# Reordering the start of the second stage of a convolution and spectral-mixing kernel

## The chip, the cores and the metric

The kernel runs on one core of one Trainium2 chip. The metric is device microseconds of that core, the median over the runs shown. A second number, the span, is the time from the first to the last instruction of one profiled execution.

## What is computed

Eight sequences of 3264 positions with 192 channels pass through a causal convolution of 7 taps (softmaxed weights, one set per head of 24 channels), then through a spectral layer that changes only the lowest 64 frequencies, and at last through a residual product with `w_ch`:

```python
x = attn(x, weight)                       # causal 7-tap convolution, per head
X = np.fft.rfft(x, axis=1)[:, :64]
Yr = einsum('bmd,mde->bme', Xr, w_r) - einsum('bmd,mde->bme', Xi, w_i)
Yi = einsum('bmd,mde->bme', Xr, w_i) + einsum('bmd,mde->bme', Xi, w_r)
y = np.fft.irfft(Y, n=S, axis=1)
u = x + y
out = u + np.maximum(u @ w_ch, 0.0)
```

## The kernel before, in words

The eight sequences are taken as four pairs, q = 0 to 3, and each sequence as 25 tiles of 128 positions (t = 0 to 24) and a half tile of 64. The program order is written out by hand, and every engine works its own queue in that order.

**Stage one** loads the inputs, convolves, transforms to 64 frequencies, and lays transposed copies of the convolved tiles into `cc`. The mixing follows: `mix(g)` (lines 430 to 441), for g = 0 to 15, multiplies four frequencies with their weights, which arrive by DMA. Its sums go to two of the four one-bank PSUM tiles `low[0]` to `low[3]`. `mix_copy` (ScalarE) takes them to SBUF, `mix_trans` transposes them into `low[2]` and `low[3]`, one bank for each half of the channels, and VectorE (the first half) and ScalarE (the second half) copy these into `yet`, the mixed spectrum.

**Stage two** is a list of items, `duos`, in the order in which they are worked. An ordinary item is a pair of output tiles for the two sequences of a q: 128 partitions and 768 columns in a PSUM tile of two banks. There are four such double tiles, and item n uses number n modulo 4. An item goes through these steps:

- `c_part` (line 488): twelve matmuls of 192 columns, the product of `cc` with `w_ch`. Its first matmul starts the accumulation, so the double tile must have been emptied of item n - 4 by then.
- `m_part(n, 0)` (line 508): the inverse transform of Y W added to it, which gives u W.
- `relu` (line 534): ScalarE, in place in PSUM.
- `m_part(n, 1)`: the inverse transform of Y added, so that PSUM holds relu(u W) + y.
- `finish` (line 559): VectorE adds x from `xall` and writes one of six output buffers in `arena`; then the output DMA is issued, on SP's queue (line 567: one DMA of 384 KB where the item is one t of two q; line 572: two of 192 KB where it is two t of one q).

Four items are not ordinary. Three of them, called Y W here, prepare the spectrum of q = 1, 2, 3: `zw_part` (line 515) multiplies `yet` by `wm` and `w1` and gives, side by side, Y W (192 columns) and Y itself (192 columns, a product with an identity matrix, part of which is zero columns); `zw_copy` scales both into `zw`. The Y W of q = 0 is done ahead of the loop, in the `low` tiles. The fourth is `"h"`, the half tiles of all sequences, written by four DMAs on POOL's queue (line 548).

The loop (lines 616 to 630) is a software pipeline. At step n it issues `m_part(n, 0)` and `relu(n)`, then `c_part(n + 1)` or the Y W that stands at n + 1, then `m_part(n - 1, 1)` and `finish(n - 1)`. Items 0 and 1 have their `c_part` ahead of the loop, item 0 behind the last mixing and item 1 behind the Y W of q = 0. The Y W items stand at places 2, 15 and 21 of the list, and `"h"` at 23. The four ring tiles of stage one close ahead of the last mixing, which frees the double tiles 0 and 1 (`za`); all four `low` tiles close behind the first Y W, which frees the double tiles 2 and 3 (`zb`).

Of the kernel before, what the change touches and what calls it, by code (L numbers as in the profile page):

```python
# [12 lines left out]
F32 = mybir.dt.float32  # L13
BF16 = mybir.dt.bfloat16
# [5 lines left out]
def kernel(  # L20
# [9 lines left out]
    nc = tc.nc  # L30
    B, S, D = x.shape
    H, KK = weight.shape
    MODES = moe_w_r.shape[0]
# [3 lines left out]
    P = 128  # L37
    NQ = B // 2
    NF = S // P
# [13 lines left out]
    def sb(name, shape, dtype, **kw):  # L53
        return pool.tile([P] + shape, dtype, tag=name, name=name, **kw)
# [15 lines left out]
    yet = sb("yet", [2, 2 * MODES, B], BF16)  # L70
# [3 lines left out]
    zw = mixa[:, 0:4 * NQ * D].rearrange("p (q c t d) -> p q c t d", q=NQ, c=2, t=2)  # L74
    band = sb("band", [H, 2 * P], BF16)
    wm = sb("wm", [2 * D], BF16)
    w1 = sb("w1", [2 * D], BF16)
# [12 lines left out]
    def wbuf(g):  # L90
        return wts[g] if g < NW + NL else wts[(g - NW - NL) % NW]
# [35 lines left out]
    def psum_pool(name, side):  # L127
        stack = ExitStack()
        return stack, stack.enter_context(tc.tile_pool(name=name, bufs=1, space=PSUM, side=side))

    conv_stack, pp = psum_pool("pconv", "left")
    Z = [pp.tile([P, 2, 512], F32, tag=f"z{i}", name=f"z{i}") for i in range(2)]
    low_stack, pp = psum_pool("plow", "right")
    low = [pp.tile([P, 512], F32, tag=f"low{i}", name=f"low{i}") for i in range(4)]

    def slot(q, t):
        return NT * q + t
# [265 lines left out]
    for k, u in enumerate(units):  # L403
# [5 lines left out]
        if k:  # L409
            q, t0, n = units[k - 1]  # L410
# [8 lines left out]
    NG = MODES // 4  # L419

    def load_w(g):
        if g < NG:
            for half, src in ((0, moe_w_r), (1, moe_w_i)):
                nc.gpsimd.dma_start(out=wbuf(g)[64 * half:64 * half + 64, :, :, :],  # L424
                                    in_=src[4 * g:4 * g + 4, :, :].rearrange("m (p j) e -> p m j e", j=3))
# [4 lines left out]
    def mix(g):  # L430
        yp = low[(g // 2) % 2][:, D * (g % 2):D * (g % 2) + D]
        for j in range(3):
            for p4 in range(4):
                m = 4 * g + p4
                nc.tensor.matmul(yp[32 * p4:32 * p4 + 2 * B, :], xt[:, j, :, m],  # L435
                                 wbuf(g)[:, p4, j, :], start=(j == 0), stop=(j == 2),
                                 tile_position=(0, 32 * p4), skip_group_check=True)
        if g < NW:
            load_w(g + NW + NL)
        elif g >= NW + NL:  # L440
            load_w(g + NW)
# [3 lines left out]
                       in_=low[d % 2][:, 0:2 * D].rearrange("p (g d) -> p g d", g=2)[:, gs, :])  # L445

    def mix_trans(d, gs=slice(0, 2)):
        ets = [low[2 + t][:, :].bitcast(BF16)[:, 0:2 * P].rearrange("p (g k) -> p g k", g=2) for t in range(2)]
        for t in range(2):
            for g in range(gs.start, gs.stop):  # L450
                nc.tensor.transpose(ets[t][:, g, :], ymix[d % 2][:, g, 64 * t:64 * t + P], ident[:])
        m = slice(8 * d + 4 * gs.start, 8 * d + 4 * gs.stop)
        for t in range(2):
            dst = yet[:, t, :, :].rearrange("p (c m) b -> p m c b", c=2)[:, m, :, :]
            srcv = ets[t][:, gs, :].rearrange("p g (q k) -> p (g q) k", q=4)[:, :, 0:16].rearrange(
                "p m (c b) -> p m c b", c=2)
            if t == 0:
                nc.vector.tensor_copy(out=dst, in_=srcv)
            else:
                nc.scalar.copy(out=dst, in_=srcv)  # L460

    conv_stack.close()
    ring_stack, pp = psum_pool("pring", "left")
# [6 lines left out]

    ROWS = (LO, UP)

    def c_part(n):
        duo, zt = items[n]
        if duo[0] == "h":
            for a in range(2):
                for j in range(3):
                    for k in range(2):
                        for i, r in enumerate(ROWS):
                            h = ROWS[i ^ k]  # L480
                            nc.tensor.matmul(zt[h, k, D * a:D * a + D], cc[r, 2 * k + a, 3 * NF + j, h], wc[r, j, :],
                                             start=(a == 0 and j == 0), stop=False, skip_group_check=True,
                                             tile_position=(r.start, h.start))
            return
        for k, (q, t) in enumerate(duo):
            for j in range(3):
                for i, r in enumerate(ROWS):
                    nc.tensor.matmul(zt[:, i, D * k:D * k + D], cc[r, q, 3 * t + j, :], wc[r, j, :],  # L488
                                     start=(k == 0 and j == 0), stop=False, skip_group_check=True)

    def m_part(n, which):

        duo, zt = items[n]
        for c in range(2):
            end = which == 1 and c == 1
            if duo[0] == "h":
                for k in range(2):
                    for i, r in enumerate(ROWS):
                        h = ROWS[i ^ k]
                        nc.tensor.matmul(zt[h, k, 0:2 * D], tabs[c][r, NF, 0:HALF], zw[r, 2 * k:2 * k + 2, c, which, :],  # L500
                                         start=False, stop=end, skip_group_check=True,
                                         tile_position=(r.start, h.start))
                continue
            (q0, t0), (q1, t1) = duo[0], duo[-1]
            parts = [(0, 2, q0, t0)] if t0 == t1 and q0 != q1 else [(k, 1, q, t) for k, (q, t) in enumerate(duo)]
            for k, w, q, t in parts:
                for i, r in enumerate(ROWS):
                    nc.tensor.matmul(zt[:, i, D * k:D * (k + w)], tabs[c][r, t, :], zw[r, q:q + w, c, which, :],  # L508
                                     start=False, stop=end and k + w == len(duo), skip_group_check=True)

    def zw_part(q, c, z):

        for t, w in enumerate((wm, w1)):
            for i, r in enumerate(ROWS):
                nc.tensor.matmul(z[r, 0:2 * D], yet[:, t, MODES * c:MODES * c + MODES, 2 * q + i], w[:],  # L515
                                 start=(t == 0), stop=(t == 1), tile_position=(0, 64 * i), skip_group_check=True)

    def zw_copy(dst, src, act):
        if act:
            nc.scalar.activation(out=dst, in_=src, func=ACT.Copy, scale=ascale[:, 0:1])  # L520
        else:
            nc.vector.tensor_scalar(out=dst, in0=src, scalar1=ascale[:, 0:1], scalar2=None, op0=ALU.mult)

    duos = [((q, t), (q, t + 1)) for q in range(2) for t in (0, 2)]
    duos += [((q, t), (q + 1, t)) for q in (0, 2) for t in range(0 if q else 4, NF)]

    duos[-1:] = [(u,) for u in duos[-1]]
    for k, item in ((2, 1), (15, 2), (21, 3), (23, ("h",))):
        duos.insert(k, item)

    def relu(n):
# [42 lines left out]
    N = len(duos)  # L574
    items = [[duo, None] for duo in duos]

    def assign(Z):
        for k, item in enumerate(items):
            if k % 4 in Z:
                item[1] = Z[k % 4]  # L580
# [14 lines left out]
    stack, pp = psum_pool("pz0", "left")  # L595
    ctx.push(stack)
    assign({k: pp.tile([P, 2, 512], F32, tag=f"za{k}", name=f"za{k}") for k in (0, 1)})
    mix(NG - 1)
    mix_copy(NG // 2 - 1, slice(1, 2))
    c_part(0)  # L600
    mix_trans(NG // 2 - 1, slice(1, 2))
    for c in range(2):
        zw_part(0, c, low[2 * c])
    for w in range(2):
        for c in range(2):
            zw_copy(zw[:, 0, c, w, :], low[2 * c][:, D * w:D * w + D], c)
    c_part(1)
    low_stack.close()
    stack, pp = psum_pool("pz1", "right")
    ctx.push(stack)  # L610
    assign({k: pp.tile([P, 2, 512], F32, tag=f"zb{k}", name=f"zb{k}") for k in (2, 3)})

    def is_duo(n):
        return 0 <= n < N and isinstance(duos[n], tuple)

    for n in range(N + 1):
        if is_duo(n):
            m_part(n, 0)
            relu(n)
        if n + 1 < N and n > 0:  # L620
            if is_duo(n + 1):
                c_part(n + 1)
            else:
                q, zt = items[n + 1]
                for c in range(2):
                    zw_part(q, c, zt[:, c, :])
                zw_copy(zw[:, q, :, :, :].rearrange("p c t d -> p c (t d)"), zt[:, :, 0:2 * D], q > 1)
        if is_duo(n - 1):
            m_part(n - 1, 1)
            finish(n - 1)  # L630


# [28 lines left out]
```

## Time and profile before

| what | value |
|---|---|
| median of 6 runs | 181.64 us (181.36 to 187.92) |
| the profiled execution | 181.42 us |
| its span | 179.7 us |
| TensorE busy in the span (PE) | 147.3 us, 82% |
| VectorE busy (DVE) | 112.0 us, 62% |
| ScalarE busy (ACT) | 98.4 us, 55% |
| stage two, first `c_part` to the last VectorE add | about 107.9 to 174.2 us |
| one ordinary item in the steady part | about 1.15 us |
| bytes written | 20.05 MB |

The profiled execution takes 1.7 us more than its span; that part lies outside the first and last instruction. Times in the views count from the start of the span. In a timeline row the columns are start, length, engine, source line, operation, output and inputs, shapes, number of instructions, and in brackets how long the engine stood idle before the row and who released it. Several instructions that follow one another are merged into one row. PEld rows are weight loads, which run beside matmuls.

### The profile page before, as it was taken

Reading aid. Unit: us, or ns where it says so; the run is one execution under the profiler, and the core shown is the slowest. Engines: PE = TensorE matmul, PEld = TensorE weight load, DVE = VectorE, ACT = ScalarE, POOL = GpSimd, SP = SyncE. Lnnn points to the kernel's source line nnn. Section 1 sums busy time; section 2 is a strip of 40 time slices with the busy share of each in tenths; the row PEclk is TensorE's granted clock in tenths of the full one; section 3 lists DMA queues with packets and bytes.
Section 4 is the critical chain, followed back from the end, with each engine's and each line's share of the span. In section 5 each row is a group of like instructions: output and inputs, shape, how many; then the busy total and the mean of one; then the engine's idle time right before and its main releaser. Section 6 shows DMA issues by size and latency. Waiting matters only on the chain.

```text
span 179.7 us, 6296 instructions
## 1 busy us (share of the span) xinstructions
PE 147.3 (82%) x2736; PEld 108.9 (61%) x2736; DVE 112.0 (62%) x159; ACT 98.4 (55%) x134; POOL 68.8 (38%) x113
## 2 busy tenths in 40 slices
PE   0047879999999997894776769999999999999940
PEld 0033556666667665673565657888776778888830
DVE  1878574866866683442435352788766878888870
ACT  8076646544554634163454455466776666666630
POOL 7999998768975644443334000000000500000000
PEclk9999999999999999699999999999999999999995
DMA  4999999999999999999999950469989699999995
GB/s 48 159 176 188 190 190 190 191 191 192 189 191 190 207 204 207 209 204 207 206 207 206 207 93 4 139 226 365 348 283 314 186 326 370 365 355 350 333 371 170
DMA packets 62875, 40.17 MB, mean 224 GB/s; under 512 B 28800, under 2 KB 62784, under 8 KB 62848
## 3 DMA queue, kind: packets, MB, share of 16 engines
q0 software_dynamic: 36224, 20.08, 80.4%
q1 hardware_dynamic: 26624, 19.69, 32.6%
q8 instruction: 21, 0.34, 0.8%
q14 instruction: 6, 0.05, 0.1%
HBM read 39.40 MB, written 20.05 MB: 331 GB/s over the span
## 4 chain that ended last, share of the span: by engine, by line
DMA 37%; PE 35%; POOL 19%; issue 3%; DVE 2%; ACT 1%; POOLq 0%; DVEq 0%
DMA arena<-in_moe_w_i_dram 18%; POOL xall L145 14%; DMA xall<-in_x_dram 13%; PE za L508 9%; PE zb L508 8%; PE za L488 8%; DMA cc<-in_moe_w_i_dram 7%; PE zb L488 6%; DVE arena L559 2%; POOL xall L215 1%; POOL arena L424 1%; PE zb L515 1%; ACT xall L321 1%; DVE arena L554 1%; PE low L435 1%
## 5 line engine op out<-in xcount | busy, mean ns | idle before, releaser
L145 POOL DMA_DIRECT2D xall<-in_x_dram x48 | 38.5, 813 | 4.7 <-DMA xall<-in_x_dram 2.3
L303 PE MATMUL z<-xall,band 64*64 64x192 bf16 (+3 forms) x816 | 27.4, 264 | 14.5 <-ACT band L189 10.5
L323 DVE CAST xall<-z 128x768 bf16<-128x768 f32 (+1 forms) x24 | 24.5, 1021 | 13.9 <-PE z L303 12.1
L303 PEld LDWEIGHTS <-band 64*64 64x64 bf16 x816 | 18.4, 110 | 22.9 <-ACT band L189 10.9
L321 ACT CAST xall<-z 128x768 bf16<-128x768 f32 (+1 forms) x24 | 20.4, 851 | 20.5 <-PE z L303 19.1
L488 PEld LDWEIGHTS <-cc 64*128 64x128 bf16 x600 | 27.0, 94 | 6.6 <-issue 1.7
L559 DVE TENSOR_TENSOR arena<-za,xall 128x768 f32<-128x768 f32 x26 | 24.8, 956 | 6.1 <-ACT za L534 2.0
L534 ACT ACTIVATE za<-za 128x768 f32<-128x768 f32 (+1 forms) x27 | 21.0, 783 | 9.5 <-PE za L508 9.5
L559 DVE TENSOR_TENSOR arena<-zb,xall 128x768 f32<-128x768 f32 x23 | 21.9, 956 | 6.3 <-ACT zb L534 2.9
L534 ACT ACTIVATE zb<-zb 128x768 f32<-128x768 f32 (+1 forms) x25 | 19.6, 782 | 10.1 <-PE zb L508 8.6
L329 PE MATMUL low<-xall,ftab 128*128 128x384 bf16 x100 | 22.0, 348 | 0.0
L383 PEld LDWEIGHTS <-xall 128*128 128x128 bf16 x300 | 18.5, 104 | 3.2 <-issue 0.3
L358 DVE COPY cc<-r 128x1024 bf16<-128x1024 bf16 (+1 forms) x16 | 10.2, 670 | 14.6 <-ACT xs L444 6.2
L548 POOL DMA_DIRECT2D out_dram<-arena x4 | 2.4, 615 | 42.4 <-DVE arena L540 42.4
L488 PE MATMUL za<-wc,cc 64*128 64x192 bf16 x318 | 17.9, 243 | 0.4 <-DVE arena L559 0.4
L508 PE MATMUL za<-mixa,ftab 64*128 64x384 bf16 (+1 forms) x120 | 18.1, 304 | 0.0
L508 PE MATMUL za<-mixa,fsin 64*128 64x384 bf16 (+1 forms) x120 | 18.1, 304 | 0.0
L508 PE MATMUL zb<-mixa,ftab 64*128 64x384 bf16 (+1 forms) x100 | 16.1, 313 | 0.4 <-ACT zb L534 0.4
L508 PE MATMUL zb<-mixa,fsin 64*128 64x384 bf16 (+1 forms) x100 | 16.1, 313 | 0.0
L488 PE MATMUL zb<-wc,cc 64*128 64x192 bf16 x282 | 15.8, 243 | 0.0
L356 ACT COPY cc<-r 128x1024 bf16<-128x1024 bf16 (+1 forms) x9 | 8.9, 989 | 10.0 <-PE r L383 8.9
L508 PEld LDWEIGHTS <-ftab 64*128 64x128 bf16 x220 | 11.8, 94 | 3.9 <-issue 1.5
(108 smaller groups left out, 185.0 us busy)
## 6 DMA issues: line engine op xcount, KB each, us to landing
out_dram<-arena SPq DMA_DIRECT2D x45, 384.0 KB, 4.4
xall<-in_x_dram POOLq DMA_DIRECT2D x24, 192.0 KB, 6.9
xall<-in_x_dram POOLq DMA_DIRECT2D x16, 240.0 KB, 6.5
arena<-in_moe_w_r_dram POOLq DMA_DIRECT2D x12, 288.0 KB, 9.2
arena<-in_moe_w_i_dram POOLq DMA_DIRECT2D x12, 288.0 KB, 10.0
out_dram<-arena SPq DMA_DIRECT2D x10, 192.0 KB, 2.8
xall<-in_x_dram POOLq DMA_DIRECT2D x8, 144.0 KB, 6.1
cc<-in_moe_w_r_dram POOLq DMA_DIRECT2D x4, 288.0 KB, 11.2
```

Of the source, the lines that this page charges most:

```text
L145: nc.gpsimd.dma_start(out=xall[:, s0:s0 + nf, i, :], in_=src)
L303: mm = nc.tensor.matmul(ov[c], band[r, h, c.start + shift + 64 * (r is UP and c is LO): c.start + shift + 64 * (r is UP and c is LO) + 64] ...
L321: nc.scalar.copy(out=dst, in_=srcv)
L323: nc.vector.tensor_copy(out=dst, in_=srcv)
L329: nc.tensor.matmul(xp, ftab[:, t, :], xall[:, slot(q, t), :, :], start=(t == 0), stop=False, skip_group_check=True)
L356: nc.scalar.copy(out=out, in_=in_)
L358: nc.vector.tensor_copy(out=out, in_=in_)
L383: nc.tensor.transpose(tp[:, P * k:P * k + P], src, ident[:])
L488: nc.tensor.matmul(zt[:, i, D * k:D * k + D], cc[r, q, 3 * t + j, :], wc[r, j, :], start=(k == 0 and j == 0), stop=False, skip_group_check ...
L508: nc.tensor.matmul(zt[:, i, D * k:D * (k + w)], tabs[c][r, t, :], zw[r, q:q + w, c, which, :], start=False, stop=end and k + w == len(duo) ...
L534: nc.scalar.activation(out=zt[:, :, 0:w], in_=zt[:, :, 0:w], func=ACT.Relu)
L559: nc.vector.tensor_tensor(out=o[:, :, :].rearrange("p k (i d) -> p i k d", i=2), in0=zt[:, :, 0:2 * D].rearrange("p i (k d) -> p i k d", k=2),
```

## The change

The diff does six things.

1. The `low` tiles are held in two pools, one with `low[1]` and `low[3]`, one with `low[0]` and `low[2]`. The second closes ahead of the last mixing, so that double tile 2 is there already; the first closes where all four closed. Only double tile 3 waits for it.
2. The transposes of the last pair of mixings put both halves of the channels into `low[3]`, side by side. The Y W of q = 0 uses `low[1]` and `low[3]`.
3. Half of `c_part(1)` (its first tile, six matmuls) is put ahead of the Y W of q = 0, the other half and the whole `c_part(2)` behind it. Before, the whole `c_part(1)` stood behind it.
4. `zw_part` leaves out the columns that are zero: three matmuls of 320, 192 and 64 columns in place of two of 384, for each of the four combinations of c and i. That makes twelve for eight, and 576 columns for 768.
5. `zw_copy` in the loop is done in two halves, Y W on VectorE and Y on ScalarE, where one instruction on one engine did both.
6. Six items, not four, take two t of one q (t = 0 to 5 of q = 0 and 1). The Y W items stand at places 3, 8 and 10, and `"h"` at 13. The loop begins with `m_part(0, 0)`, `m_part(1, 0)`, `m_part(2, 0)`, the Y W of q = 1, and only then `m_part(0, 1)` and `m_part(1, 1)`, each with its `finish`; the step behind them is `c_part(4)`.

```diff
-    low_stack, pp = psum_pool("plow", "right")
-    low = [pp.tile([P, 512], F32, tag=f"low{i}", name=f"low{i}") for i in range(4)]
+    low = [None] * 4
+    low_stacks = []
+    for odd in (1, 0):
+        stack, pp = psum_pool(f"plow{odd}", "right")
+        low_stacks.append(stack)
+        for i in (odd, odd + 2):
+            low[i] = pp.tile([P, 512], F32, tag=f"low{i}", name=f"low{i}")
...
-        ets = [low[2 + t][:, :].bitcast(BF16)[:, 0:2 * P].rearrange("p (g k) -> p g k", g=2) for t in range(2)]
+        ets = [(low[3][:, P * t:P * t + P] if d == NG // 2 - 1 else low[2 + t][:, 0:P]).bitcast(BF16).rearrange(
+            "p (g k) -> p g k", g=2) for t in range(2)]
...
-        for t, w in enumerate((wm, w1)):
+        for t, w, e0, e1 in ((0, wm, 0, D + P), (1, w1, 0, D), (1, w1, D + P, 2 * D)):
             for i, r in enumerate(ROWS):
-                nc.tensor.matmul(z[r, 0:2 * D], yet[:, t, MODES * c:MODES * c + MODES, 2 * q + i], w[:],
-                                 start=(t == 0), stop=(t == 1), tile_position=(0, 64 * i), skip_group_check=True)
+                nc.tensor.matmul(z[r, e0:e1], yet[:, t, MODES * c:MODES * c + MODES, 2 * q + i], w[:, e0:e1],
+                                 start=(t == 0), stop=(e1 == 2 * D), tile_position=(0, 64 * i),
+                                 skip_group_check=True)
...
-    duos = [((q, t), (q, t + 1)) for q in range(2) for t in (0, 2)]
-    duos += [((q, t), (q + 1, t)) for q in (0, 2) for t in range(0 if q else 4, NF)]
+    duos = [((q, t), (q, t + 1)) for q in range(2) for t in (0, 2, 4)]
+    duos += [((q, t), (q + 1, t)) for q in (0, 2) for t in range(0 if q else 6, NF)]
...
-    for k, item in ((2, 1), (15, 2), (21, 3), (23, ("h",))):
+    for k, item in ((3, 1), (8, 2), (10, 3), (13, ("h",))):
...
+    low_stacks.pop().close()
+    stack, pp = psum_pool("pz1", "left")
+    ctx.push(stack)
+    assign({2: pp.tile([P, 2, 512], F32, tag="zb", name="zb")})
     mix(NG - 1)
     mix_copy(NG // 2 - 1, slice(1, 2))
     c_part(0)
     mix_trans(NG // 2 - 1, slice(1, 2))
+    c_part(1, (0,))
     for c in range(2):
-        zw_part(0, c, low[2 * c])
+        zw_part(0, c, low[2 * c + 1])
...
-    c_part(1)
-    low_stack.close()
-    stack, pp = psum_pool("pz1", "right")
+    c_part(1, (1,))
+    c_part(2)
+    low_stacks.pop().close()
+    stack, pp = psum_pool("pz2", "right")
...
-        if n + 1 < N and n > 0:
+        if n + 1 < N and n > 1:
...
-                zw_copy(zw[:, q, :, :, :].rearrange("p c t d -> p c (t d)"), zt[:, :, 0:2 * D], q > 1)
-        if is_duo(n - 1):
-            m_part(n - 1, 1)
-            finish(n - 1)
+                for w in range(2):
+                    zw_copy(zw[:, q, :, w, :], zt[:, :, D * w:D * w + D], w)
+
+        for k in {1: (), 2: (0, 1)}.get(n, (n - 1,)):
+            if is_duo(k):
+                m_part(k, 1)
+                finish(k)
```

More of the change, by code (lines that the diff above doesn't have):

```diff
@@ L471, with c_part @@
     ROWS = (LO, UP)
-    def c_part(n):
+    def c_part(n, ks=(0, 1)):
         duo, zt = items[n]
@@ L485, in c_part @@
         for k, (q, t) in enumerate(duo):
-            for j in range(3):
+            for j in range(3) if k in ks else ():
                 for i, r in enumerate(ROWS):
@@ L601 @@
     mix_trans(NG // 2 - 1, slice(1, 2))
+    c_part(1, (0,))
     for c in range(2):
-        zw_part(0, c, low[2 * c])
+        zw_part(0, c, low[2 * c + 1])
     for w in range(2):
         for c in range(2):
-            zw_copy(zw[:, 0, c, w, :], low[2 * c][:, D * w:D * w + D], c)
-    c_part(1)
-    low_stack.close()
-    stack, pp = psum_pool("pz1", "right")
+            zw_copy(zw[:, 0, c, w, :], low[2 * c + 1][:, D * w:D * w + D], c)
+    c_part(1, (1,))
+    c_part(2)
+    low_stacks.pop().close()
+    stack, pp = psum_pool("pz2", "right")
     ctx.push(stack)
-    assign({k: pp.tile([P, 2, 512], F32, tag=f"zb{k}", name=f"zb{k}") for k in (2, 3)})
+    assign({3: pp.tile([P, 2, 512], F32, tag="zc", name="zc")})
     def is_duo(n):
```

## The prediction

> **What bounds the kernel now.** I read the chain of waits first. From 107.5 us on it is nearly all TensorE, line 488 and line 508 in turn; before that it is input DMAs, which the change does not touch. So the question is what TensorE does between the last mixing and its last matmul. The timeline of the start answers that:
>
> ```profile
> 107.91 0.67 PE L488 MATMUL za<-wc,cc 64*128 64x192 bf16 x12
> 108.51 0.28 PE L451 MATMUL low<-ident,xs 128*128 128x128 bf16 x2
> 109.02 0.44 PE L515 MATMUL low<-wm,yet 128*64 128x384 bf16 x2 [0.23 <-DVE yet L458]
> 109.88 0.67 PE L488 MATMUL za<-wc,cc 64*128 64x192 bf16 x12
> 111.14 0.44 PE L515 MATMUL zb<-wm,yet 128*64 128x384 bf16 x2
> 111.42 0.33 PE L515 MATMUL zb<-w,yet 128*64 128x384 bf16 x2
> 111.58 0.33 PE L515 MATMUL zb<-wm,yet 128*64 128x384 bf16 x2
> 111.74 0.33 PE L515 MATMUL zb<-w,yet 128*64 128x384 bf16 x2
> 112.00 0.11 PEld L508 LDWEIGHTS <-ftab 64*128 64x128 bf16 x4 [0.22 <-issue]
> 112.17 1.02 DVE L522 TENSOR_SCALAR mixa<-zb,ascale 128x768 bf16<-128x768 f32 x1 [1.66 <-PE zb L515]
> 113.11 1.81 DVE L559 TENSOR_TENSOR arena<-za,xall 128x768 f32<-128x768 f32 x2
> 114.11 0.67 PE L488 MATMUL za<-wc,cc 64*128 64x192 bf16 x12 [0.36 <-DVE arena L559]
> ```
>
> The two holes in it are 0.23 us ahead of the first Y W (it waits for `yet`) and the one ahead of 114.11, where `c_part(4)` waits until `finish(0)` has emptied its double tile; `finish(0)` stood behind the 1.02 us copy of Y W on VectorE. TensorE's stream ended about 113.57, so that hole is 0.54. From 116 on an item follows every 1.15 us: `c_part` 0.49 and two `m_part` of 0.325, with ACT and DVE idle about 0.35 and 0.19 in each.
>
> The table by stretches says whether the output transfers matter instead (after the busy times: granted clock, DMA share, GB/s):
>
> ```profile
> 158.00:160.00 2.00, 2.00 (x40) 1.66 (x36) 1.74 (x2) 1.56 (x2) 0.00 (x0) 1.00 1.10 365
> 162.00:164.00 2.00, 2.00 (x38) 1.65 (x36) 1.62 (x3) 1.30 (x3) 0.00 (x0) 1.00 0.99 331
> 168.00:170.00 2.00, 2.00 (x41) 1.68 (x37) 1.68 (x2) 1.30 (x3) 0.00 (x0) 1.00 0.88 293
> 174.00:176.00 2.00, 0.00 (x0) 0.00 (x0) 0.16 (x1) 0.00 (x0) 0.00 (x0) 0.96 1.09 371
> ```
>
> The writes' ceiling is about 371 GB/s, 1.06 us for 393,216 bytes; an item every 1.15 us asks for 343. The rate falls below the ceiling at 162 and 168: the queue has caught up. A shift of TensorE's start therefore reaches the end nearly whole.
>
> **What the Trainium skill says.** "TensorE: Matmul & The Clock Gate", Step-by-step, has weight loads pulled ahead of running matmuls, so that they cost nothing while the matmul in front lasts longer. The trace agrees with a limit: in Y W the pairs follow at 0.16, their 384 columns, but the first step is 0.27 to 0.28; an uncovered load of `yet` costs 0.11. "TensorEngine Tiling (Array Packing)", Key Properties: "Changing tiling mode (not just tile) drains the TensorE". The trace shows 0.10 between the end of one stream and the other kind of matmul (111.74 plus 0.16 is 111.90; the next begins 112.00). "PSUM — Partial Sum Buffer", PSUM bank collisions: two engines must not touch one bank and quadrant at once, two readers included. So I count the new pairs of copies out of one bank as one after the other; the trace before has no such pair. "Perfetto Trace Analysis", Optimizing Scalar/DVE Operations: each instruction has a fixed price. It agrees: VectorE's copy takes 412 ns for 192 columns and 1016 for 768, so 1.05 ns a column and about 0.21 fixed, and 0.61 for 384.
>
> **The change, part by part.**
>
> *Y W without zero columns* (four times). At 0.417 ns a column (0.16 for 384) the three pairs stream 0.133, 0.08 and 0.027. But each pair loads its own weights, the third the same again, and a load of 0.11 cannot hide behind 0.08 or 0.027. Sum for two c: 0.11 first load, then 0.133, 0.11, 0.11, 0.133, 0.11 and the last 0.027: 0.73. Before: 0.11 and four times 0.16, 0.75. With the switch behind it 0.84 against 0.86: the columns saved come back as loads. Bounds: 0.70 if loads hide wholly; 1.05 if no step falls below 0.16.
>
> *Half of `c_part(1)` in the first hole.* The transposes' stream ends at 108.63; a switch 0.10, six matmuls 0.25, a switch 0.10: Y W at 109.08. VectorE's copy of `yet` now waits for both transposes (0.06 later) and ScalarE's for VectorE's, but its half is wanted only behind the first pair, at 109.33. I take 109.10, 0.08 later than before, with 0.25 of work done in it. Bounds: 109.02 and 109.30.
>
> *Up to the first `finish`.* Y W 0.84, the rest of `c_part(1)` and `c_part(2)` 0.74, three `m_part` 0.98, a switch 0.10: the second Y W begins at 111.76 (before 111.14), `m_part(0, 1)` at 112.60 (112.00). VectorE's copy begins 1.03 behind the Y W's start, less 0.02: 112.77. It now lasts 0.61, with the next instruction 0.08 into it: `finish(0)` can start at 113.30; by TensorE it could at 113.19 (0.59 behind `m_part`). So VectorE still decides, by a little. It takes 0.96, and 0.05 later `c_part(4)` starts: **114.31 against 114.11**. TensorE is through `m_part(1, 1)` at 113.25 and stands idle 1.06, not 0.54. By then both kernels have done the same: three `c_part`, five `m_part`, two Y W. So the start costs 0.20, for all that was moved into the hole: it lengthened the way to `finish(0)` by as much as it did work.
>
> *Next items.* Before, `c_part(5)` waited 0.04 for `finish(1)`. Now `m_part(2, 1)` goes first (114.80), so `finish(2)` runs 115.39 to 116.35 and `c_part(6)`, ready at 116.27, starts at 116.40: 0.13. That is 0.09 more.
>
> *Y W of q = 2, 3 earlier.* Before, `c_part` waited about 0.12 and 0.05 behind the one of q = 2. Now it delays `m_part(6, 1)` and with it `finish(6)`, for which the Y W of q = 3, two places on, waits about 0.1, and the next `c_part` waits about 0.06 for `finish(7)`: even. Shorter Y W: minus 0.04 for two. Halved copies: ScalarE's half waits for VectorE's, ending 0.2 later than one copy did, but the double tile is wanted again only four items on. ScalarE's queue behind it holds the next `relu`, over 0.3 later.
>
> *DMAs.* SP issues 12 and not 8 halves of 192 KB (0.38 to 0.5 each, so about 0.95 an item, below 1.15), and 43 and not 45 whole ones. The POOL issues of `"h"` (four of 0.62) move from 140.4 to about 128; POOL is idle 42 us ahead of them. With them moves the slow stretch of the writes (138 to 146 us, 196 to 285 GB/s). What hides it are the items behind it, 41 now: each leaves the writes 0.09 us (1.15 less 1.06) to catch up, 3.5 us in all. I count nothing, at most 0.3.
>
> **Sum:** 0.20 + 0.09 − 0.04 = +0.25 us. The profiled execution had 181.42 (span 179.7 and 1.7 around it), so 181.67; the median lies 0.22 above it: **181.9 us**.
>
> **Rivals.**
> *Loads rule Y W (slower).* Twelve loads for eight, and no step under 0.16: Y W is 1.05, 0.19 more, not 0.02 less; four times 0.21 on top of 0.25 is about +1.0: **182.6**. It crosses the line of 0.3% where a load takes over about 0.14. For it: PEld L515 lasts 199 ns on average, L488's 94. Against: the uncovered load showed 0.11 only.
> *Loads hide (faster).* Y W is 0.70: four times 0.14 less, 0.25 − 0.56: **181.3**; with the half `c_part` quite free (0.08) and VectorE's half copy no longer in front of `finish(0)` (0.11) 181.1. For it: line 372's loads of 128x64 lie under steps of 0.056. Against: these read neighbours, `yet` every eighth element, and only they show the 0.11.
> *Nothing arrives.* Writes at the end lag by about 0.6 us behind the last issue; if they set the end, a later start is swallowed: **181.6**. Against: the dip at 168.
>
> **From cases to numbers.** About 0.3%, 0.54 us, is what a measurement here can tell from no change. Even (my sum or nothing arriving), 0.50; slower rival, or the sum with a load of over 0.14 or one switch more, 0.36; faster, 0.14. Their bounds run from 181.1 to 182.6; I give 181.1 to 182.8, the top for a switch and a wait more.
>
> **What would show it.** Right: a hole of about 1 us ahead of `c_part(4)`, which starts near 114.3; steps of about 0.11 behind the 192- and 64-column pairs of Y W; six matmuls of `c_part` between transposes and Y W; 1.15 an item unchanged. Wrong: `c_part(4)` before 114.0, Y W at 0.7 or over 1.0, or an item time that has moved.

## The result and the profile after

| | before | after |
|---|---|---|
| median in the same comparison | 181.47 us (65 runs) | 182.67 us (30 runs, 181.58 to 184.18) |
| the profiled execution | 181.42 us, span 179.7 | 183.09 us, span 181.1 |
| ratio after to before | | 1.0072, 95% interval 1.0057 to 1.0086 |

The changed kernel is slower by 0.72%, and the interval lies clear of no change. Some executions of any version run at a lower granted clock and take a per cent or more longer; the ratios leave them out, the medians do not.

The spans of the two profiled executions differ by 1.40 us. The span of every run is on record too: its median is 180.75 for after (30 runs), and 179.65 to 179.8 for before in the three comparisons of the experiments. So about 1.0 of the 1.2 us lies in the span. The rest lies outside it, where before took 1.72 to 1.85 in each of these runs, and after 1.72 to 2.58, median 1.95; no run here shows why.

I split the two profiled spans at points that both traces have:

| stretch | before | after | difference | forecast |
|---|---|---|---|---|
| start of the span to the start of the last mixing | 107.51 | 107.36 | −0.15 | 0 |
| last mixing to the start of `c_part(4)` | 6.59 | 7.00 | +0.41 | +0.20 |
| the next items, to the end of the fourth `finish` | | | +0.11 | +0.09 |
| items behind it, the Y W of q = 2, 3 and `"h"` among them | | | +0.15 | −0.04 |
| hole in TensorE behind `"h"` | 0.21 | 0.57 | +0.36 | 0, at most 0.3 |
| start of the last matmul to the landing of the last output packet | 5.42 | 5.56 | +0.14 | 0 |
| last landing to the end of the span | 1.24 | 1.62 | +0.38 | 0 |

The first row lies ahead of everything that the change touches. The row of the last landing varied by 0.5 between the kernels below without an edit there (5.03 in e1, 5.53 in e8), so I read nothing from it. The others are four separate places, the start, `"h"`, the hole behind it and the end. Below, **path** is the time from the start of the last mixing to the start of the last matmul: 65.49 before, 66.52 after.

**The start.** The timeline of the kernel after, columns as in the one of before:

```profile
107.75 0.67 PE L495 MATMUL za<-wc,cc 64*128 64x192 bf16 x12
108.35 0.28 PE L458 MATMUL low<-ident,xs 128*128 128x128 bf16 x2
108.56 0.42 PE L495 MATMUL za<-wc,cc 64*128 64x192 bf16 x6
108.74 0.19 DVE L465 COPY yet<-low 128x64 bf16<-128x64 bf16 x1 [1.71 <-PE low L458]
108.96 0.21 ACT L467 COPY yet<-low 128x64 bf16<-128x64 bf16 x1 [0.78 <-DVE yet L465]
108.99 0.41 PE L522 MATMUL low<-wm,yet 128*64 128x320 bf16 x2
109.23 0.42 PE L522 MATMUL low<-w,yet 128*64 128x192 bf16 x4
...
109.96 0.42 PE L495 MATMUL za<-wc,cc 64*128 64x192 bf16 x6
...
111.80 0.41 PE L522 MATMUL zc<-wm,yet 128*64 128x320 bf16 x2
112.05 0.31 PE L522 MATMUL zc<-w,yet 128*64 128x192 bf16 x4
112.19 0.39 PE L522 MATMUL zc<-wm,yet 128*64 128x320 bf16 x2
112.42 0.31 PE L522 MATMUL zc<-w,yet 128*64 128x192 bf16 x4
112.66 0.34 PE L515 MATMUL za<-mixa,ftab 64*128 64x192 bf16 x4
112.83 0.62 DVE L530 TENSOR_SCALAR mixa<-zc,ascale 128x384 bf16<-128x384 f32 x1 [2.29 <-ACT za L542]
113.36 1.81 DVE L567 TENSOR_TENSOR arena<-za,xall 128x768 f32<-128x768 f32 x2
114.36 0.67 PE L495 MATMUL za<-wc,cc 64*128 64x192 bf16 x12 [0.87 <-DVE arena L567]
```

The six matmuls of line 495 at 108.56 fill the first hole, as intended. But the copies into `yet` now follow one another: ScalarE's begins at 108.96, where VectorE's (108.74 plus 0.19) has ended, and it ends at 109.17. The second pair of Y W needs it and starts at 109.23. From 108.99 to 109.96 this Y W takes 0.97, while the one at 111.80 takes 0.86, to 112.66. From there on it goes as foretold: VectorE's half copy of the second Y W at 112.83 for 0.62, `finish(0)` at 113.36, `c_part(4)` at 114.36. TensorE's stream stood still 1.03 ahead of it, against 0.52 before.

**Around `"h"`.** The same view, TensorE's rows alone; lines 488 and 507 are the half tiles, in 64 by 64 pieces:

```profile
124.38 0.69 PE L488 MATMUL za<-wc,cc 64*64 64x192 bf16 x24
125.00 0.34 PE L515 MATMUL zc<-mixa,ftab 64*128 64x384 bf16 x2
125.17 0.33 PE L515 MATMUL zc<-mixa,fsin 64*128 64x384 bf16 x2
125.43 0.36 PE L507 MATMUL za<-mixa,ftab 64*64 64x384 bf16 x4
125.62 0.33 PE L507 MATMUL za<-mixa,fsin 64*64 64x384 bf16 x4
125.88 0.67 PE L495 MATMUL zb<-wc,cc 64*128 64x192 bf16 x12
```

Between the two steps of the half tiles stands the `m_part(11, 1)` of an ordinary item, in 64 by 128 pieces. TensorE changes its tiling there and back, 0.09 to 0.11 each time: six changes around `"h"`, where before had four, because there the item two places ahead of `"h"` was a Y W, which has no `m_part`, and the two steps touch (136.37 less 135.87 is 0.50, all stream):

```profile
135.87 0.69 PE L481 MATMUL zb<-wc,cc 64*64 64x192 bf16 x24
136.37 0.36 PE L500 MATMUL zb<-mixa,ftab 64*64 64x384 bf16 x4
136.53 0.36 PE L500 MATMUL zb<-mixa,fsin 64*64 64x384 bf16 x4
136.82 0.67 PE L488 MATMUL za<-wc,cc 64*128 64x192 bf16 x12
```

**Behind `"h"`.** Six items later:

```profile
129.51 2.43 POOL L556 DMA_DIRECT2D out_dram<-arena  x4 [31.59 <-DVE arena L548]
...
135.99 0.96 DVE L567 TENSOR_TENSOR arena<-zc,xall 128x768 f32<-128x768 f32 x1 [0.95 <-DMA out_dram<-arena]
137.00 0.67 PE L495 MATMUL zc<-wc,cc 64*128 64x192 bf16 x12 [0.41 <-DVE arena L567]
```

The `finish` at 135.99 wants the output buffer that `"h"` filled. It waits 0.95 for the last of the four transfers issued from 129.51 on, and line 495 waits for it. The table of waits gives both (columns: engine, buffer and line, for whom; total us, how often, longest):

```profile
DVE arena L567 <- DMA out_dram<-arena: 1.0, 1, 1.0
PE zc L495 <- DVE arena L567: 0.4, 1, 0.4
```

Before had a wait of the same kind, 0.6 long:

```profile
DVE arena L559 <- DMA out_dram<-arena: 0.6, 1, 0.6
```

**The writes.** The table by stretches, columns as before:

```profile
136.00:138.00 2.00, 1.59 (x28) 1.09 (x26) 1.81 (x2) 1.08 (x2) 0.00 (x0) 1.00 1.10 370
160.00:162.00 2.00, 2.00 (x40) 1.68 (x37) 1.76 (x2) 1.54 (x2) 0.00 (x0) 1.00 0.85 278
168.00:170.00 2.00, 2.00 (x40) 1.70 (x38) 1.77 (x2) 1.52 (x2) 0.00 (x0) 1.00 0.75 247
```

In the first row TensorE is busy 1.59 of 2.00: the hole. The dips to 278 and 247 GB/s with TensorE always busy say that the queue is drained there. So the cover of 41 items was enough for the writes, and a delay of TensorE reaches the end.

**The end of the kernel.** SP closes the program by waiting for the eight semaphores of its DMA queue, one after the other in a fixed order. The waits of SP from 173 us on, first of before, then of after:

```profile
SPq L656 <- DMA out_dram<-arena: 3.3, 5, 1.0
```

```profile
SPq L673 <- DMA out_dram<-arena: 3.8, 2, 3.3
```

Before, the transfers ended in the order in which SP asks, so it waits five times, at most 1.0, and is done when the last one lands. After, the two that are signalled last are the first and the second in its order. It waits 3.3 for the first and about 0.5 more for the second, the last of all; six others follow at about 0.06 each, though they have long been signalled: the 0.38 of the table. Which semaphore is signalled last follows from the number of output DMAs on SP's queue, each of which takes the next of the eight in turn. One input DMA on that queue has taken the first, so that 55 outputs end on the eighth, and 57 on the second. The page's table of issues gives 57 for the kernel after (43 and 14; size of each, us to landing), where before has 55:

```profile
out_dram<-arena SPq DMA_DIRECT2D x43, 384.0 KB, 4.3
...
out_dram<-arena SPq DMA_DIRECT2D x14, 192.0 KB, 3.0
```

### The profile page after: what moved, and what is told of

It reads as the page before. It is cut to its first block, busy times and chain, and to the rows that moved or that the text cites. A ratio compares the mean times of both kernels' runs of the same rounds, so it can differ in the third digit from the quotient of the medians.

```text
span 181.1 us, 6367 instructions
## 1 busy us (share of the span) xinstructions
PE 146.7 (81%) x2768; PEld 109.4 (60%) x2768; DVE 112.9 (62%) x161; ACT 98.2 (54%) x135; POOL 68.8 (38%) x113
## 4 chain that ended last, share of the span: by engine, by line
DMA 39%; PE 30%; POOL 19%; issue 4%; DVE 3%; DVEq 0%; POOLq 0%
DMA arena<-in_moe_w_i_dram 18%; POOL xall L150 14%; DMA xall<-in_x_dram 12%; PE za L515 7%; DMA cc<-in_moe_w_i_dram 7%; PE za L495 6%; PE zb L515 4%; PE zc L515 3%; PE zc L495 3%; PE zb L495 3%; DMA out_dram<-arena 3%; DVE arena L567 2%; POOL arena L429 1%; POOL xall L220 1%; POOL out_dram L556 1%
## 5 line engine op out<-in xcount | busy, mean ns | idle before, releaser
L567 DVE TENSOR_TENSOR arena<-za,xall 128x768 f32<-128x768 f32 x25 | 23.8, 956 | 5.4 <-PE za L515 2.2
L495 PE MATMUL za<-wc,cc 64*128 64x192 bf16 x306 | 17.4, 243 | 0.9 <-DVE arena L567 0.9
L515 PE MATMUL za<-mixa,ftab 64*128 64x384 bf16 (+1 forms) x120 | 17.4, 299 | 0.0
L515 PE MATMUL za<-mixa,fsin 64*128 64x384 bf16 (+1 forms) x120 | 17.4, 299 | 0.0
L567 DVE TENSOR_TENSOR arena<-zc,xall 128x768 f32<-128x768 f32 x12 | 11.5, 956 | 3.7 <-ACT za L542 1.5
L515 PEld LDWEIGHTS <-fsin 64*128 64x128 bf16 x228 | 12.1, 94 | 2.2
L429 POOL DMA_DIRECT2D arena<-in_moe_w_r_dram x12 | 7.4, 615 | 15.7 <-PE low L440 10.6
L567 DVE TENSOR_TENSOR arena<-zb,xall 128x768 f32<-128x768 f32 x12 | 11.5, 956 | 2.3 <-ACT zc L542 2.0
L542 ACT ACTIVATE zb<-zb 128x768 f32<-128x768 f32 (+1 forms) x13 | 10.0, 771 | 4.6 <-PE zb L515 4.6
```

Source lines behind the costliest of these rows:

```text
L542: nc.scalar.activation(out=zt[:, :, 0:w], in_=zt[:, :, 0:w], func=ACT.Relu)
L567: nc.vector.tensor_tensor(out=o[:, :, :].rearrange("p k (i d) -> p i k d", i=2), in0=zt[:, :, 0:2 * D].rearrange("p i (k d) -> p i k d", k=2),
```

## The experiments

Times of this table are medians, ratios are to before on the same chip. Path, hole (TensorE's, behind `"h"`) and end (last landing to the end of the span) are read from the one profiled execution of each; `c_part(4)` counts from the start of the last mixing.

| kernel | us | before | ratio, 95% | path | hole | path without hole | end | `c_part(4)` |
|---|---|---|---|---|---|---|---|---|
| before | 181.47 | | | 65.49 | 0.21 | 65.28 | 1.24 | 6.59 |
| after | 182.67 | 181.47 | 1.0072 (1.0057 to 1.0086) | 66.52 | 0.57 | 65.95 | 1.62 | 7.00 |
| e1_full_columns | 182.41 | 181.51 | 1.0058 (1.0042 to 1.0074) | 66.11 | 0.19 | 65.92 | 1.63 | 6.97 |
| e2_h_at_12 | 182.34 | 181.51 | 1.0053 (1.0034 to 1.0071) | 65.92 | 0.24 | 65.68 | 1.62 | 7.01 |
| e3_seven_buffers | 183.15 | 181.51 | 1.0075 (1.0044 to 1.0107) | 65.93 | none | 65.93 | 1.59 | 7.01 |
| e4_two_banks | 182.54 | 181.51 | 1.0058 (1.0037 to 1.0078) | 66.17 | 0.29 | 65.88 | 1.61 | 6.93 |
| e5_last_on_118 | 182.23 | 181.44 | 1.0048 (1.0027 to 1.0068) | 66.50 | 0.54 | 65.96 | 1.24 | 7.01 |
| e6_before_57 | 181.71 | 181.44 | 1.0018 (1.0001 to 1.0035) | 65.50 | 0.21 | 65.29 | 1.61 | 6.59 |
| e7_m21_first | 182.57 | 181.44 | 1.0065 (1.0042 to 1.0088) | 66.11 | 0.54 | 65.57 | 1.62 | 7.01 |
| e8_late_places | 183.36 | 181.44 | 1.0107 (1.0074 to 1.0140) | 66.53 | 0.62 | 65.91 | 1.61 | 7.01 |
| e9_one_copy | 182.76 | 181.63 | 1.0075 (1.0050 to 1.0100) | 66.63 | 0.31 | 66.32 | 1.62 | 7.41 |
| e10_four_repairs | 181.55 | 181.63 | 0.9992 (0.9968 to 1.0016) | 65.34 | 0.12 | 65.22 | 1.26 | 6.94 |
| e11_repairs_seven | 181.67 | 181.63 | 1.0010 (0.9978 to 1.0042) | 65.20 | none | 65.20 | 1.23 | 6.93 |
| e12_before_seven | 181.29 | 181.63 | 0.9978 (0.9959 to 0.9996) | 65.28 | none | 65.28 | 1.23 | 6.59 |

The path without the hole repeats well: where nothing was edited in it, it lies within 0.02 of its parent (e5 and e3 to after, e6 and e12 to before). One repair of 0.1 to 0.4 us is at or below what the times resolve; the trace judges those, and the times judge the sum.

**e1: the zero columns put back** (into the kernel after).

```diff
-        for t, w, e0, e1 in ((0, wm, 0, D + P), (1, w1, 0, D), (1, w1, D + P, 2 * D)):
+        for t, w, e0, e1 in ((0, wm, 0, 2 * D), (1, w1, 0, 2 * D)):
```

> The changed kernel, but each Y W of q = 0 to 3 with the two matmuls of 384 columns again in place of three of 320, 192 and 64. Theory (weight loads of yet set the pace of the short pairs): no difference to the changed kernel, +1.2 us over before; a Y W inside the loop takes 0.86 us to the next matmul as with three. Rival (streamed columns set it): each Y W is 0.16 us longer, +1.8 us over before. Rival (twelve loads are the new cost): each Y W is 0.1 to 0.2 us shorter, +0.6 over before.

Its Y W of q = 1, TensorE's rows of the timeline, up to the next step:

```profile
111.55 0.44 PE L522 MATMUL zc<-wm,yet 128*64 128x384 bf16 x2
111.82 0.33 PE L522 MATMUL zc<-w,yet 128*64 128x384 bf16 x2
111.98 0.33 PE L522 MATMUL zc<-wm,yet 128*64 128x384 bf16 x2
112.15 0.33 PE L522 MATMUL zc<-w,yet 128*64 128x384 bf16 x2
112.41 0.34 PE L515 MATMUL za<-mixa,ftab 64*128 64x192 bf16 x4
```

From 111.55 to 112.41 is 0.86, with 768 columns and eight loads; the kernel after has 0.86 with 576 columns and twelve. So this part of the change is neutral: what the removed columns gave, the four added loads took back. The Trainium skill ("TensorE: Matmul & The Clock Gate", Step-by-step) has the next weights loaded while a matmul runs; here a load of about 0.11 stands behind only 0.08 or 0.027 of streaming (estimates, from 0.16 for 384 columns), so that part of it must show. That is the reading of the sum. Pair by pair the rows of after do not place it: the 192 and 64 columns together take 0.14 (112.05 to 112.19), the 320 behind them 0.23.

**e2: `"h"` one place earlier**, two places behind the Y W of q = 3.

```diff
-    for k, item in ((3, 1), (8, 2), (10, 3), (13, ("h",))):
+    for k, item in ((3, 1), (8, 2), (10, 3), (12, ("h",))):
```

> The changed kernel, but the half-tile item h at place 12 of the list, not 13, so that its c_part and its first m_part stand next to each other (no m_part of another item between, because place 10 is a Y W and has none at step 11). Theory (two more changes of the tiling mode at 0.09 us): TensorE's sum of gaps around h falls by 0.18, +1.0 us over before. Rival (the place of h costs nothing): +1.2 over before.

```profile
123.82 0.69 PE L488 MATMUL za<-wc,cc 64*64 64x192 bf16 x24
124.33 0.33 PE L507 MATMUL za<-mixa,ftab 64*64 64x384 bf16 x4
124.50 0.33 PE L507 MATMUL za<-mixa,fsin 64*64 64x384 bf16 x4
124.76 0.67 PE L495 MATMUL za<-wc,cc 64*128 64x192 bf16 x12
```

In its timeline the two steps of the half tiles now touch (123.82 and 124.33: 0.51, all stream), and the path without the hole falls by 0.27. Two changes of tiling at 0.09 to 0.11 explain 0.18 to 0.22 of it, and the gap ahead of `"h"` is about 0.03 smaller. That each change empties TensorE is what the Trainium skill says ("TensorEngine Tiling (Array Packing)", Key Properties); the price is from these traces.

**e3: a seventh output buffer**, in `band`, which is not used any more in stage two.

```diff
-    NO = 6
+    NO, NA = 7, 6
+    more = band[:, :, :].rearrange("p h c -> p (h c)")
...
-    outs = [arena[:, OB * i:OB * (i + 1)].bitcast(F32).rearrange("p (k d) -> p k d", k=2) for i in range(NO)]
+    outs = [a[:, OB * i:OB * (i + 1)].bitcast(F32).rearrange("p (k d) -> p k d", k=2)
+            for a, m in ((arena, NA), (more, NO - NA)) for i in range(m)]
```

> The changed kernel with a seventh output buffer, laid over band, which nothing reads any more in the second stage. Theory (finish of the item six places behind h waits for the slow DMAs of h, and TensorE loses 0.57 us there): VectorE no longer waits for a DMA, the hole of TensorE near 136 us is gone, +0.6 to +0.8 us over before. Rival (the writes set the end, and the wait only shows their backlog): the hole is gone but the writes' backlog is longer at the end, +1.2 over before.

The hole is gone and nothing else in the path moved: the wait for the buffer of `"h"` was its cause. The time did not follow: 183.15 from 9 runs, with a wide interval, and the profiled execution, with a span of 180.2, is the shortest of the nine (median 180.8; after has 180.75). From the last matmul to the last landing it has 5.71 against 5.56, within the scatter of that row. Whether the writes take back what the hole gave is open from this run; e11 and e12 come back to it.

**e4: the two halves of the last transposes in two banks**, so that the copies need not take turns.

```diff
-        ets = [(low[3][:, P * t:P * t + P] if d == NG // 2 - 1 else low[2 + t][:, 0:P]).bitcast(BF16).rearrange(
+        ets = [(low[1 if t and gs.start else 3][:, 3 * P * t if gs.start else P * t:][:, 0:P] if d == NG // 2 - 1
+                else low[2 + t][:, 0:P]).bitcast(BF16).rearrange(
```

> The changed kernel, but the last transposes put their second half into low[1], behind its 384 columns, so that VectorE's and ScalarE's copies into yet read different banks and can run at once. Theory (the second copy waits for the first, and the second pair of the first Y W then has its weight load uncovered, 0.11 us): the first Y W takes 0.86 and not 0.97 us, c_part(4) starts 6.9 us behind the last mixing, not 7.0, +1.1 us over before. Rival (the copy from one bank was hidden, as predicted): c_part(4) stays at 7.0, +1.2.

The copies now run side by side: in the timeline VectorE's starts at 110.40 and ScalarE's at 110.39.

```profile
110.39 0.21 ACT L467 COPY yet<-low 128x64 bf16<-128x64 bf16 x1 [0.48 <-PE low L458]
110.40 0.19 DVE L465 COPY yet<-low 128x64 bf16<-128x64 bf16 x1 [1.66 <-PE low L458]
```

The first Y W now takes 0.86 (110.74 to 111.60), so the 0.11 that it had lost came from the serial copies. It starts 0.04 later, so that `c_part(4)` comes 0.07 earlier.

**e5: sixty-three output DMAs in place of 57**, so that the last one again takes the semaphore that SP asks for last.

```diff
+        if n in range(30, 36):
+            for k in range(2):
+                dst = bass.AP(tensor=out.tensor, offset=out.offset + (2 * (q0 + k) * S + P * t0) * D,
+                              ap=[[D, P], [S * D, 2], [1, D]])
+                nc.sync.dma_start(out=dst, in_=ov[:, 2 * k:2 * k + 2, :])
-        if t0 == t1:
+        elif t0 == t1:
```

> The changed kernel, but the outputs of the items 30 to 35 go out in two DMAs of 192 KB each instead of one of 384 KB, so that SP issues 63 output DMAs, not 57, and the last one signals semaphore 118 again, as before, not 112. Theory (SP waits for the eight semaphores one after the other at the end, 0.06 us each; after the last landing the changed kernel has six more of these waits to do): the time from the last landing to the end of the span falls from 1.6 to 1.24 us, +0.7 us over before. Rival (the end is the same, the longer tail in the profiles is chance): 1.6 stays, +1.1 over before.

**e6: the reverse, in the kernel before.** The same edit there with `n in (34, 35)`: 57 output DMAs, nothing else.

> The kernel before, but the outputs of the items 34 and 35 go out in two DMAs of 192 KB each, so that SP issues 57 output DMAs and the last signals semaphore 112, as in the changed kernel. Theory (the number of DMAs sets how many waits are left behind the last landing): the time from the last landing to the end of the span rises from 1.24 to 1.6 us, +0.37 us over before. Rival (it belongs to the reordering, not to the number of DMAs): 1.24 stays and the time is that of before.

SP's waits from 173 us on, first of e5, then of e6:

```profile
SPq L678 <- DMA out_dram<-arena: 3.2, 5, 1.0
```

```profile
SPq L661 <- DMA out_dram<-arena: 3.6, 2, 3.1
```

The pattern of waits changes sides with the number of DMAs, and the end with it: 1.24 in e5, 1.61 in e6, the path in both unmoved (0.02 and 0.01). e6 is slower than before by 0.18% (0.01% to 0.35%), about 0.3 us of the 0.37 seen in the trace. For e5 the interval of the time overlaps that of after, but the spans of all its runs agree with the trace: median 180.3, where after has 180.75.

**e7: `m_part(2, 1)` and `finish(2)` ahead of `c_part(4)`**, into the hole of 1.03.

```diff
+        if n == 3:
+            m_part(2, 1)
+            finish(2)
...
-        for k in {1: (), 2: (0, 1)}.get(n, (n - 1,)):
+        for k in {1: (), 2: (0, 1), 3: ()}.get(n, (n - 1,)):
```

> The changed kernel, but at step 3 m_part(2, 1) and finish(2) stand ahead of c_part(4). Theory (the hole ahead of c_part(4) waits for finish(0) alone, and this m_part needs only the relu of its own item, over at about 113.5): the hole shrinks from 1.03 to about 0.7 us in two pieces, c_part(4) still starts 7.0 us behind the last mixing, finish(2) comes earlier and c_part(6) no longer waits 0.13; +0.75 us over before. Rival (it is the chain of finishes on VectorE that sets the pace there, and it stays): the hole moves to c_part(6) or further, +1.1 over before.

```profile
113.49 0.34 PE L515 MATMUL zb<-mixa,ftab 64*128 64x192 bf16 x4
113.65 0.34 PE L515 MATMUL zb<-mixa,fsin 64*128 64x192 bf16 x4
114.29 0.67 PE L495 MATMUL za<-wc,cc 64*128 64x192 bf16 x12 [0.30 <-DVE arena L567]
115.02 0.95 DVE L567 TENSOR_TENSOR arena<-zb,xall 128x768 f32<-128x768 f32 x1
```

In the timeline the step of 0.33 stands in the hole at 113.49, `c_part(4)` is as late as in after (7.01 behind the mixing), and `finish(2)` begins at 115.02, so `c_part(6)` waits 0.04 and not 0.13. The path without the hole falls by 0.38. So TensorE had work for this hole all along; the new order of the first steps left it empty. The median, 182.57, doesn't resolve this gain.

**e8: the Y W items and `"h"` back at their late places**, everything else as in after.

```diff
-    for k, item in ((3, 1), (8, 2), (10, 3), (13, ("h",))):
+    for k, item in ((3, 1), (15, 2), (21, 3), (23, ("h",))):
```

> The changed kernel, but only the first Y W of the loop stays at place 3; the other two and h stand at 15, 21 and 23 as before. Theory (early places cost only by the two extra changes of the tiling mode around h): TensorE's path is 0.2 us shorter than that of the changed kernel, as with h at 12, +0.9 over before; c_part(4) is where it is in the changed kernel. Rival (early places crowd the start, and the start is dear because of them): +0.4 or less over before.

Neither theory holds. With `"h"` two places behind a Y W again, two changes of tiling go, and still the path without the hole is only 0.04 below after, 0.23 above e2, which differs in the places alone. In its timeline TensorE waits 0.16 and 0.05 behind the Y W of q = 2, and 0.06 ahead of `"h"` beside the change of tiling; e2 waits 0.05 at its early Y W items. So the early places are worth about 0.2 if `"h"` stands two places behind a Y W. Most of what e8 keeps of the loss is the start: its fourth `finish` ends as late as that of after, 0.52 behind before's. Its time, from six runs, is above that of after, but the intervals overlap.

**e9: one copy of Y W in the loop** in place of the two halves.

```diff
-                for w in range(2):
-                    zw_copy(zw[:, q, :, w, :], zt[:, :, D * w:D * w + D], w)
+                zw_copy(zw[:, q, :, :, :].rearrange("p c t d -> p c (t d)"), zt[:, :, 0:2 * D], q > 1)
```

> The changed kernel, but the Y W of the loop is copied to zw by one instruction on one engine again (VectorE for q = 1, ScalarE for q = 2 and 3). Theory (VectorE's copy stands ahead of finish(0), which c_part(4) waits for): the copy takes 1.02 and not 0.62 us, c_part(4) starts about 0.4 us later, 7.4 behind the last mixing, and the end 0.4 later, +1.6 us over before. Rival (the halves cost as much as they save, since ScalarE's half waits for VectorE's): the end is that of the changed kernel, +1.2.

In its timeline VectorE's copy ahead of `finish(0)` is the long one again:

```profile
113.64 1.02 DVE L530 TENSOR_SCALAR mixa<-zc,ascale 128x768 bf16<-128x768 f32 x1 [2.28 <-ACT za L542]
```

1.02 against 0.62 is 0.40, and `c_part(4)` starts 0.40 later (7.41 for 7.00). VectorE is what decides the start of `c_part(4)`, and the halving is a good part of the change: without it the start would lose 0.81 and not 0.41. The time does not show it: 0.75% over before, where after has 0.72%, is what the rival foretold. In the profiled execution the path is only 0.11 longer than that of after, because the hole behind `"h"` is 0.26 smaller.

**e10: four repairs together** (e2, e4, e5, e7). **e11: the same with the seventh buffer. e12: the kernel before with the seventh buffer** (the edit of e3).

> The changed kernel with four repairs at once: h at place 12, the last copies of yet out of two banks, m_part(2, 1) and finish(2) ahead of c_part(4), and six outputs split so that the last DMA signals semaphore 118. Theory (the costs add up: 0.27, 0.07 and 0.38 of TensorE's path and 0.37 of the end): TensorE's path from the last mixing is that of before within 0.1, 65.3 us apart from the hole behind h, and the time is that of before within 0.2 us. Rival (a cost that none of the runs so far has shown): +0.5 us or more over before is left.

> The same four repairs and a seventh output buffer laid over band. Theory (the wait of finish for the slow DMAs of h costs TensorE 0.2 to 0.6 us, and TensorE's path sets the end): 0.2 to 0.5 us less than with the four repairs alone, 0.2 under before. Rival (the writes' backlog at the end takes what the buffer gives): as with the four repairs alone.

> The kernel before with a seventh output buffer laid over band. Theory: TensorE's hole of 0.21 us behind h is gone, 0.2 us less than before. Rival (the writes' backlog takes it): no difference.

The three path terms subtracted from after give 65.95 − 0.27 − 0.07 − 0.38 = 65.23; e10 has 65.22. Its end is 1.26, and its time equals before's: 0.9992 (0.9968 to 1.0016), an interval that lies wholly below that of after. The repairs add up, and the loss is gone. Two things in this are no repair of a cause: `c_part(4)` is still at 6.94, 0.35 behind before, and e7 makes up for that by filling the wait; and the hole is 0.12, 0.45 below that of after, though none of the four edits was aimed at it. e11 takes the rest of the hole away (0.12) and gains nothing that the times resolve. e12 is the only version that beats before, and by little: the hole of 0.21 goes, and the time falls by 0.22% (0.04% to 0.41%), about 0.1 to 0.7 us, which takes in 0.21; the median of its spans, 179.5, is 0.3 below before's beside it. That a hole removed behind `"h"` reaches the end is seen there and not in e3.

**Open.** The hole behind `"h"` has two sizes where `"h"` stands at the place of after: 0.19 to 0.31 in e1, e4 and e9, and 0.54 to 0.57 in after, e5 and e7. (With `"h"` elsewhere it is 0.24 in e2, 0.12 in e10 and 0.62 in e8.) In the traces the last of the four transfers of `"h"` lands 5.9 to 6.1 us behind the first issue where the hole is small, and 6.3 to 6.4 where it is large. The chip does not separate them: e5, e7 and e9 ran on one chip. So the 0.36 by which the hole grew is that of one execution, and no run shows that the change itself makes the hole larger; what slows the transfers is not settled.

## Why the prediction was right and wrong

The direction of the sum was right, +0.25, and the size too small: the likeliest case said no measurable change, the result is slower. The time, 182.67, lies in the range, near its top, which had been set "for a switch and a wait more"; both came, but the sum had neither, and about 0.2 of the rise lies outside the span. The failed steps are these.

*Y W without zero columns: −0.02 each; measured 0.00.* The sum, columns paid back as loads, was right, and e1 shows it; the steps of 0.11 behind the short pairs, named as a sign, are not in the rows. The slower rival, no step under 0.16 and Y W at 1.05, and the faster one, 0.70, were both wrong: 0.86. The third of the rivals, nothing arrives, was wrong too: the path's loss is in the span, and the queue is drained at 168.

*The first hole: +0.08; measured +0.12, and 0.11 more in the first Y W.* Here I had the serial copies, but judged the second one hidden, since "its half is wanted only behind the first pair". What is wanted there is not the matmul but its weight load, and that must begin before the first pair has ended. With the copy ending at 109.17, the second pair starts at 109.23 and its load lies bare. Together with that the start cost 0.41 and not 0.20. By the clock of the span `c_part(4)` came at 114.36 for a forecast of 114.31, but that is luck: the mixing began 0.15 earlier.

*The hole ahead of `c_part(4)` and the next item* were right: 1.03 for 1.06; VectorE's copy at 112.83 for 0.62 (forecast 112.77 for 0.61); `c_part(6)` waits 0.13 (0.13); an item stays at 1.15.

*`"h"`: counted at nothing.* Its DMAs were priced, its neighbours were not: what stands two places ahead of it decides whether an `m_part` of another tiling falls between its two steps. Two more changes of tiling, 0.18 to 0.22 by the gaps, 0.27 by e2: with them the −0.04 of this stretch became +0.15. The case "one switch more" stood among the rivals, but without a place in the list of items.

*DMAs: nothing, at most 0.3; measured 0.36 in the profiled execution.* The mechanism was looked for in the wrong place, in SP's issues and in the writes at the end, which caught up as foretold. The wait is that of one `finish` for the buffer of `"h"`. A hole of the same kind was there before (0.21), so it should have had a line in the sum. How much of the growth belongs to the change stays open, since e1, e4 and e9 have 0.19 to 0.31.

*Around the span and at its end: taken as constant.* The 1.7 around the span was 1.95 in the median of after. The stretch behind the last landing had no term; the number of output DMAs, which I had counted, moves it by 0.37 to 0.38. Nothing in the profile of before shows that as a cost; the wait at the end looks like one for the last transfer.

## What to carry to other kernels

When steps are moved in a software pipeline, write out what is issued ahead of and behind each special item at its new place: changes of tiling and the buffers that it holds come with the place, not with the item. A copy that feeds a matmul is due when the weight load must begin, not when the matmul does. And when an edit changes the number of DMAs, compare the stretch behind the last landing before anything else is explained.

## What the runs showed of the hardware that was not expected

- The end of the program took up to 0.37 us more or less with the number of DMAs on the output queue: 1.23 to 1.26 with 55 and 63, 1.59 to 1.63 with 57 (all fourteen kernels; e5 and e6 change nothing else).
- A change of tiling took 0.09 to 0.11 us between 64 by 128, 128 by 64 and 64 by 64 pieces, each way.
- A load of 64 columns of `yet`, elements eight apart, shows 0.11 us where nothing covers it, and twelve matmuls with 576 columns in all took as long as eight with 768 (0.86 us for Y W in both forms).
